# Sigmoid attention and a gated layer on one core: order of the visits, sums issued ahead, and fewer weights converted beside the attention

## The chip, the cores and the metric

The kernel runs on one core of a Trainium2 chip. A core has TensorE (PE, matmuls, and PEld for its weight loads), VectorE (DVE), ScalarE (ACT), GpSimd (POOL) and SyncE (SP), which here only issues transfers. The metric is the device time of one execution in microseconds; lower is better.

## The reference

```python
# q, k, v: (8, 12, 448, 64); w_gate, w_val: (768, 1536); w_out: (1536, 768)
scores = q @ k.T / sqrt(64) - log(448)
x = sigmoid(scores) @ v                 # per batch and head; heads joined: x is (8*448, 768)
gate = sigmoid(x @ w_gate)
y = (gate * (x @ w_val)) @ w_out        # (3584, 768)
```

The weights arrive in float64 and are converted to float32 in the kernel, from their 64-bit words.

## The kernel before, in words

**Attention.** 24 head groups `m` with 7 steps `g` each make 168 beats. In a beat TensorE makes one tile of scores (L314) and the values of an earlier one (L331); ScalarE makes the sigmoid (L317). A finished pair of heads is evicted by a ScalarE copy (L341) and a VectorE addition (L348), which frees its PSUM tile, and goes to `x_dram`.

**Conversion of weights.** `convert` is a generator of steps. A group of 12 steps (`operands`) takes four blocks of 128x384 words through integer operations on VectorE and POOL (`Words.first`, `Words.second`), forms seven operands of Strassen's product (`high`, and the four sums at L193), splits each into a high part rounded to the fp32r type (POOL, L157) and the rest as a low part (VectorE, L143), and stores it (`a_dram` for the first layer, `o_ops` for the output layer). The first layer needs 12 groups: `jp` = 0 to 5, each with `t` = 0 (gate) and 1 (value). In the attention 10 of them are done (`FIRST_JPS = 5`; 120 steps spread over 160 beats), the other two and the six groups of the output layer run beside the visits, by a table `due` that says how many steps follow each product (tick).

**Visits.** The batch of 8 is treated as 4 pairs. An "A" visit makes the first layer of a pair, a "C" visit its output layer, each by Strassen-Winograd's seven products. All visits use matmuls of 128x128 by 128x448 in fp32r, three for each product of tiles (low weight by high x, high by high, high by low).

An A visit has 12 units of 7 products, 84 products of 9 matmuls. Its operands are the seven combinations of x, as high and low parts `bh`, `bl` (`bs`). They are made by `split_x`: a cast on ScalarE (L244), a subtraction on VectorE (L217), and the sums of x on POOL (L217). `load_x` loads the next pair's x into `r` tiles beside the visit, and `split_x` for the next visit runs beside the last unit, three steps for each product. Products are added up by `plus` (L428, VectorE from PSUM, POOL from SBUF), gates are taken by ScalarE (L484), values multiplied by the gate on VectorE or POOL (L583).

A C visit has n = 0 to 6 with three products each of 18 matmuls. Its operands `hh`, `hl` are made by `Operands`: `make` runs the generator on, a cast on ScalarE (L520), a subtraction on VectorE (L217) and sums in place on POOL (L217), issued at the step before the cast of the item that needs them. `OPERANDS = 10` tiles of each kind hold them.

The hidden rows of a pair are either held in SBUF (`hold`, tiles `v`), where the C visit follows the A visit at once, or stored (`h<-g`) and read back during the C visit before (`load_hidden`, `hx<-h`, `v<-h`).

Weight operands come from memory through a ring of 8 tiles `A` (`load_operands`, L279), each loaded when the product that used its tile is done. Of the first layer's operands 15 stay resident in the `v` tiles and in `res`, loaded in the first A visit and used again in the second.

SyncE issues all transfers in program order. Every engine works through its own instructions in order; so the order in which the program emits steps is the order in each queue.

The order of visits before is the line

```python
visits = [("A", 0), ("A", 1), ("A", 2), ("C", 2), ("A", 3), ("C", 3), ("C", 1), ("C", 0)]
```

Of the kernel before, what the change touches and what calls it, by code (L numbers as in the profile page):

```python
# [9 lines left out]
F32 = mybir.dt.float32  # L10
# [8 lines left out]
P = 128  # L19
# [6 lines left out]

AHEAD, AHEAD_FF = 4, 2

FIRST_JPS = 5

LAG = 2

RING = 8
BEYOND = 3

OPERANDS = 10


@with_exitstack
def sigmoid_attention_glu_kernel(ctx: ExitStack, tc: tile.TileContext, qk, v, wg, wv, wo, out):  # L40
# [43 lines left out]
    o_ops = [dram.tile([KC, P, KH, 2, P], F32, name=f"oo{n}") for n in range(N_OPS)]  # L84
    h_dram = {}

    def chunks(jps, ks):
        res = []
        for jp in jps:
            for w in (wg, wv):  # L90
                res += [w[2 * jp + j][:, c * CW:(c + 1) * CW] for j in range(2) for c in range(2)]
        for k in ks:
            res += [wo[k + KH * half][:, c * CW:(c + 1) * CW] for c in range(2) for half in range(2)]
        return res
# [35 lines left out]
            nc.vector.scalar_tensor_tensor(out=m, in0=raw[:, :, 0], scalar=21, in1=m, op0=ALU.logical_shift_right, op1=ALU.bitwise_or)  # L130
            nc.vector.scalar_tensor_tensor(out=f, in0=m, scalar=2.0 ** -31, in1=f, op0=ALU.mult, op1=ALU.mult)  # L131

    def convert(words, jps, ks):

        pool = words.pool

        unsent, unsplit = [], []

        def split(keep):

            while len(unsplit) > keep:
                to, hl, key, sends = unsplit.pop(0)
                nc.vector.tensor_tensor(out=hl[:, 1], in0=to, in1=hl[:, 0], op=ALU.subtract)  # L143
                unsent.append((key, sends))

        def send(keep):

            while len(unsent) > keep:
                key, sends = unsent.pop(0)
                for s in sends:  # L150
                    nc.sync.dma_start(**s)
                stored.add(key)

        def high(to, where):
            key, sends = where
            hl = pool.tile([P, 2, CW], F32R, tag="whl", name="whl", bufs=words.held)
            nc.gpsimd.tensor_copy(hl[:, 0], to)  # L157
            unsplit.append((to, hl, key, sends(hl.bitcast(F32))))

        def to_a(jp, t, n):  # L160
            return ("a", jp, t, n), lambda hl: [dict(out=a_dram[jp][t][n], in_=hl)]

        def to_op(k, n):
            return ("o", k, n), lambda hl: [dict(out=o_ops[n][:, :, k, a].rearrange("o p f -> p o f"),
                                                 in_=hl[:, a].rearrange("p (o f) -> p o f", f=P)) for a in range(2)]

        def chunk(i, where, done):
            f = pool.tile([P, CW], F32, tag=f"wf{i}", name="wf", bufs=1)
            done.append(f)
            words.first(f)  # L170
            split(1)
            send(1)
            yield
            send(0)
            split(0)
            words.second()
            if where:
                high(f, where)
            yield

        def operands(to):
            fs = []
            for i, n in enumerate((0, 4, None, 6)):
                yield from chunk(i, to(n) if n is not None else None, fs)
            a11, a12, a21, a22 = fs
            split(0)

            s2 = pool.tile([P, CW], F32, tag="wf4", name="wf", bufs=1)
            for n, (x, y, z, op) in enumerate(((a22, a21, a22, ALU.add), (s2, a22, a11, ALU.subtract),
                                                (a21, a11, a21, ALU.subtract), (a12, a12, s2, ALU.subtract))):  # L190
                split(1)
                send(1)
                nc.gpsimd.tensor_tensor(out=x, in0=y, in1=z, op=op)  # L193
                high(x, to((1, 2, 3, 5)[n]))
                yield

        for jp in jps:
            for t in range(2):
                yield from operands(lambda n: to_a(jp, t, n))
        for k in ks:  # L200
            yield from operands(lambda n: to_op(k, n))
        split(0)
        send(0)
# [7 lines left out]
        return xpool.tile([P, S], F32, tag=tag, name=tag)  # L211

    pairs = list(range(B // 2))
    visits = [("A", 0), ("A", 1), ("A", 2), ("C", 2), ("A", 3), ("C", 3), ("C", 1), ("C", 0)]

    def subtract(engine, to, x, y):
        engine.tensor_tensor(out=to, in0=x, in1=y, op=ALU.subtract)  # L217
# [1 line left out]
    def load_x(pr, new):  # L219
# [4 lines left out]
            nc.sync.dma_start(out=xs[i, k], in_=x_dram[i // 2 * KC + k][:, b * S:(b + 1) * S])  # L224
            yield
        for k in range(KC):
            xs[4, k] = new()
            subtract(nc.gpsimd, xs[4, k], xs[1, k], xs[0, k])
            yield
            subtract(nc.gpsimd, xs[1, k], xs[3, k], xs[1, k])  # L230
            yield

    def split_x(cast=nc.scalar.copy):

        work = [(n, k) for n in range(N_OPS) for k in range(KC)]
        source = lambda n, k: xs[(0, 4, 4, 1, 2, 3, 4)[n], k]
        for at in range(len(work) + 2):
            if at >= 2:
                hi, lo = bs[work[at - 2]]
                subtract(nc.vector, lo, source(*work[at - 2]), hi)  # L240
            if 1 <= at <= len(work):
                n, k = work[at - 1]
                bs[n, k] = tuple(xpool.tile([P, S], F32R, tag=f"b{a}{n}{k}", name=f"b{a}") for a in "hl")
                cast(bs[n, k][0], source(n, k))  # L244
            if at < len(work):
                n, k = work[at]
                if n in (2, 6):
                    subtract(nc.gpsimd, xs[4, k], xs[3 if n == 2 else 2, k], xs[4, k])
            yield


    N_A = 2 * JPS * N_OPS
    RESIDENT = range(12, N_A, 5)
    N_HELD = 2 * KH

    def visit_operands(v_):
        kind, _ = visits[v_]
        if kind == "A":
            return [(a_dram[jp][t][n].rearrange("p a f -> p (a f)"), [("a", jp, t, n)],
                     r if r in RESIDENT and v_ < 2 else None)  # L260
                    for r, (jp, t, n) in enumerate(itertools.product(range(JPS), range(2), range(N_OPS)))]
        return [(o_ops[n][o][:, h * KC:(h + 1) * KC].rearrange("p k a f -> p (k a f)"),
                 [("o", h * KC + k, n) for k in range(KC)], None) for n in range(N_OPS) for o in range(KC) for h in range(2)]
# [26 lines left out]
    with tc.manual_schedule(), tc.tile_pool(name="att", bufs=2) as att, tc.tile_pool(name="sc", bufs=2, space=PSUM) as scp, \  # L290
# [82 lines left out]
        nc.vector.memset(zeros, 0.0)  # L373
        load_first()
        warm_up(2)
        words = Words(att, chunks(range(FIRST_JPS), ()), AHEAD, 4)
        weights, n_weights, done = convert(words, range(FIRST_JPS), ()), 24 * FIRST_JPS, 0

        first_x = 2 * NQ + 1
        tags = iter(SUMS)  # L380
        x_loads = load_x(0, lambda: sb(next(tags)) if len(xs) < len(SUMS) else att.tile([P, S], F32, tag=f"xt{len(xs)}", name="xt", bufs=1))
        splits = split_x(nc.gpsimd.tensor_copy)
        beat = 0
        for m in range(B * NQ):
# [29 lines left out]


    hid = ctx.enter_context(tc.tile_pool(name="hid", bufs=1, reuse_waits="tile"))
    rawx = ctx.enter_context(tc.tile_pool(name="rawx", bufs=1, reuse_waits="tile"))
    un = ctx.enter_context(tc.tile_pool(name="un", bufs=8, space=PSUM, reuse_waits="tile"))

    later = []  # L420
# [79 lines left out]
    class Operands:  # L500
# [6 lines left out]
        def steps(self):  # L507
# [4 lines left out]
            for at in range(len(self.items) + 2):  # L512
                if at >= 2:
                    item = self.items[at - 2]
                    subtract(nc.vector, hb[item][1], source(*item), hb[item][0])
                if 1 <= at <= len(self.items):
                    assert at - 1 < self.used + OPERANDS
                    item = self.items[at - 1]
                    hb[item] = tuple(oper[0].tile([P, S], F32R, tag=f"h{a}", name=f"h{a}", bufs=OPERANDS) for a in "hl")
                    nc.scalar.copy(hb[item][0], source(*item))  # L520
                if at < len(self.items):
                    pr, n, k = self.items[at]
                    b = [hs.get((pr, i, k)) for i in range(4)]
                    sums = {1: (b[0], b[1], b[0]), 2: (b[0], b[3], b[0]), 3: (b[1], b[3], b[1]), 6: (b[0], b[2], b[0])}
                    if n in sums:
                        subtract(nc.gpsimd, *sums[n])
                yield

        def make(self, to):
# [7 lines left out]

    def new_raw():
        raw_names[0] += 1
        return rawx.tile([P, S], F32, tag=f"r{raw_names[0] % (5 * KC)}", name="r")  # L540

    def a_visit(v_):

# [10 lines left out]
        def tick():  # L554
# [7 lines left out]
            if p >= N_A - 6:  # L562
                for _ in range(3):
                    next(splits, None)
                if keep:
                    chain[0].make(min(2 * (p - (N_A - 7)), OPERANDS + 1))
            beside(v_, p)

        for jp in range(JPS):
# [27 lines left out]
    def load_hidden(pr):  # L597

        def new(at):
            if visits[-1][1] == pr:  # L600
                return held(at).bitcast(F32)
            return [xpool.tile([P, S], F32, tag=f"b{a}{at // KC}{at % KC}", name="hx") for a in "hl"]

# [8 lines left out]
    def c_visit(v_):  # L612
# [14 lines left out]
        for n in range(N_OPS):  # L627
            ops.make(ops.used + KH + 2)
            for o in range(KC):
# [13 lines left out]
                    nc.scalar.copy(p5, acc)  # L643
                elif n == 2:
                    plus(u2, acc, p1)
                    plus(u4, u2, p5, nc.gpsimd)
                elif n == 3:
                    plus(u2, acc, u2)
                    plus(p5, u2, p5, nc.gpsimd)
                    send(1, 1, p5)  # L650
                elif n:
                    to, m, t = {4: (p1, 0, 0), 5: (u4, 0, 1), 6: (u2, 1, 0)}[n]
                    plus(to, acc, to)
                    send(m, t, to)
                if o < KC - 1:
                    ops.make(ops.used + OPERANDS + o)
                next(splits, None)
                if steps % 6 == 0:
                    next(splits, None)
# [8 lines left out]
    stage = ExitStack()  # L668
    stage.enter_context(tc.manual_schedule())
    conv = stage.enter_context(tc.tile_pool(name="conv", bufs=1, reuse_waits="tile"))  # L670
    res = stage.enter_context(tc.tile_pool(name="res", bufs=1, reuse_waits="tile"))

    def make_resident():
# [4 lines left out]

    new_resident[0] = make_resident

    words = Words(conv, chunks(range(FIRST_JPS, JPS), range(KH)), AHEAD_FF, 3)
    weights = convert(words, range(FIRST_JPS, JPS), range(KH))
    n_first, n_second = 24 * (JPS - FIRST_JPS), 12 * KH
    last_conv = 2
    quiet = [t for v_ in range(last_conv) for t in range(N_A * (v_ + 1) - 7, N_A * (v_ + 1) + 8)]
    firsts = range(5, 49)
    seconds = [t for t in range(49, N_A * (last_conv + 1) - 16) if t not in quiet]
    due = {}
    for ticks, n in ((firsts, n_first), (seconds, n_second)):
        for i, t in enumerate(ticks):  # L690
# [54 lines left out]
```

## Time and profile before

| | |
|---|---|
| median of 3 runs | 1235.29 us (1234.97 to 1235.72) |
| the profiled execution | 1232.44 us, its span 1230.7 us |
| mean granted TensorE clock | 0.992 |
| busy, share of the span | PE 97%, weight loads 80%, DVE 65%, ACT 34%, POOL 49% |
| matmuls | 2688 records in the attention, 4536 in the visits, 16 to warm up |
| transfers | 359.60 MB, mean 292 GB/s |

Places in the span (us): attention to 270; A0 270 to 427; A1 427 to 587; A2 587 to 746; C2 746 to 833; A3 to 991; C3 to 1071; C1 to 1151; C0 to the end. Tables by stretch give, for each window, its length, then each engine's busy time with the number of its records in brackets, the granted clock, the share of the transfer engines and their rate. In rows of groups the numbers behind the bar are busy time, the mean of one in ns, and the idle time of the engine before them with what ended it.

### The profile page before, as it was taken

How to read it: one execution, taken by the hardware profiler on the slowest of the kernel's cores; microseconds unless marked ns; L12 is line 12 of the kernel's file. 1: busy time of each engine (PE TensorE's matmuls, PEld its weight loads, DVE VectorE, ACT ScalarE, POOL GpSimd, SP SyncE). 2: the span in 40 equal slices, each digit the busy share in tenths (PEclk: the TensorE clock that was granted, in tenths of full speed). 3: DMA queues.
4: the chain of work that ended last, by engine and by line, in shares of the span. 5: the costliest groups of instructions: out<-in, count | busy, mean ns of one | idle time of the engine just before them, and what ended most of it. 6: DMA issues, size and time to landing. Idle time of an engine off the chain costs nothing. (4 is left out here: it accounts for less than half of the span.)

```text
span 1230.7 us, 20521 instructions
## 1 busy us (share of the span) xinstructions
PE 1199.8 (97%) x7240; PEld 983.8 (80%) x7240; DVE 805.7 (65%) x1208; ACT 423.7 (34%) x664; POOL 608.8 (49%) x607
## 2 busy tenths in 40 slices
PE   9999999999999989999999999899999999999998
PEld 4444464459999979999899998789999998988988
DVE  6887789956688586877776756763232466556563
ACT  6777676561111321122311224421112233233231
POOL 3334556544564644654648438632222277353651
PEclk9999999999999999999999999889999999999999
DMA  9999999989999769999699997578777788989876
GB/s 324 359 367 410 328 330 312 332 283 353 398 353 370 238 246 367 296 319 300 231 377 312 302 280 209 161 222 255 217 214 217 216 267 283 355 279 321 290 201 195
DMA packets 168343, 359.60 MB, mean 292 GB/s; under 512 B 16305, under 2 KB 79409, under 8 KB 168241
## 3 DMA queue, kind: packets, MB, share of 16 engines
q1 hardware_dynamic: 168240, 358.28, 87.4%
q8 instruction: 58, 0.95, 0.3%
q14 instruction: 45, 0.36, 0.1%
HBM read 275.64 MB, written 82.58 MB: 291 GB/s over the span
## 5 line engine op out<-in xcount | busy, mean ns | idle before, releaser
L443 PE MATMUL un<-bh,A 128*128 128x448 f32 x1836 | 523.9, 367 | 0.0
L443 PEld LDWEIGHTS un<-bh,A 128*128 128x128 f32 x1836 | 345.6, 188 | 29.8 <-issue 0.7
L443 PE MATMUL un<-bl,A 128*128 128x448 f32 x918 | 337.3, 367 | 5.8 <-DVE bl L217 5.8
L443 PE MATMUL un<-hh,A 128*128 128x448 f32 x1008 | 290.6, 370 | 4.9 <-ACT hh L520 4.9
L331 PE MATMUL av<-a,v 64*64 64x448 f32 x1344 | 208.3, 540 | 7.1 <-DVE x L348 7.0
L443 PEld LDWEIGHTS un<-hh,A 128*128 128x128 f32 x1008 | 192.0, 191 | 21.1 <-ACT hh L520 6.1
L314 PE MATMUL sc<-qk 64*64 64x448 f32 x1344 | 207.0, 541 | 0.4 <-ACT a L317 0.4
L317 ACT ACTIVATE a<-sc,bias 128x896 f32<-128x896 f32 x168 | 169.3, 1009 | 78.3 <-PE sc L314 67.9
L443 PE MATMUL un<-hl,A 128*128 128x448 f32 x504 | 188.7, 374 | 7.6 <-DVE hl L217 7.5
L443 PEld LDWEIGHTS un<-bl,A 128*128 128x128 f32 x918 | 172.8, 188 | 22.9 <-DVE bl L217 8.5
L157 POOL CAST whl<-wf 128x384 fp32r<-128x384 f32 x126 | 71.7, 569 | 176.4 <-DVE wf L131 119.7
L428 POOL TENSOR_TENSOR u<-u,p 128x448 f32<-128x448 f32 x48 | 57.2, 1192 | 197.0 <-DVE u L428 196.7
L217 DVE TENSOR_TENSOR hl<-v,hh 128x448 fp32r<-128x448 f32 x126 | 120.4, 989 | 32.3 <-ACT hh L520 27.3
L331 PEld LDWEIGHTS av<-a,v 64*64 64x64 f32 x1344 | 76.9, 134 | 69.4 <-issue 49.7
L314 PEld LDWEIGHTS sc<-qk 64*64 64x64 f32 x1344 | 75.9, 134 | 69.3 <-issue 55.4
L143 DVE TENSOR_TENSOR whl<-wf,whl 128x384 fp32r<-128x384 f32 x126 | 111.8, 891 | 25.5 <-POOL whl L157 25.3
L484 ACT ACTIVATE g<-c 128x448 f32<-128x448 f32 x96 | 52.6, 575 | 201.3 <-DVE c L428 169.2
L443 PEld LDWEIGHTS un<-hl,A 128*128 128x128 f32 x504 | 95.9, 190 | 23.4 <-DVE hl L217 16.0
L217 POOL TENSOR_TENSOR v<-v 128x448 f32<-128x448 f32 x72 | 99.8, 1413 | 22.1 <-DVE hl L217 21.1
L520 ACT CAST hh<-v 128x448 fp32r<-128x448 f32 x126 | 67.8, 567 | 113.0 <-PE un L443 66.8
L456 ACT COPY p<-un 128x448 f32<-128x448 f32 x48 | 25.4, 529 | 224.2 <-PE un L443 203.0
L428 DVE TENSOR_TENSOR u<-un,p 128x448 f32<-128x448 f32 x48 | 29.8, 622 | 98.2 <-PE un L443 97.4
(70 smaller groups left out, 1239.0 us busy)
## 6 DMA issues: line engine op xcount, KB each, us to landing
A<-ad SPq DMA_DIRECT2D x306, 384.0 KB, 4.8
A<-oo SPq DMA_DIRECT2D x168, 384.0 KB, 4.1
ad<-whl SPq DMA_DIRECT2D x84, 384.0 KB, 6.4
qk<-qk SPq DMA_DIRECT2D x23, 896.0 KB, 7.4
oo<-whl SPq DMA_DIRECT2D x84, 192.0 KB, 5.6
v<-vv SPq DMA_DIRECT2D x24, 448.0 KB, 6.8
xd<-x SPq DMA_DIRECT2D x48, 224.0 KB, 6.9
h<-g SPq DMA_DIRECT2D x48, 224.0 KB, 4.8
```

The costliest lines, as they stand in the source:

```text
L143: nc.vector.tensor_tensor(out=hl[:, 1], in0=to, in1=hl[:, 0], op=ALU.subtract)
L157: nc.gpsimd.tensor_copy(hl[:, 0], to)
L217: engine.tensor_tensor(out=to, in0=x, in1=y, op=ALU.subtract)
L314: nc.tensor.matmul(sc[halves[u], h, :S], lhsT=qkt[halves[h], p, k0:k0 + HP], rhs=qkt[halves[h], p, :S], start=True, stop=True)
L317: nc.scalar.activation(a, sc[:, :, :S], AF.Sigmoid, bias=bias, scale=scale)
L331: nc.tensor.matmul(avs[key][halves[h], :S], lhsT=vt[halves[u], g, h], rhs=a[halves[u], h], start=start, stop=g == last)
L428: engine.tensor_tensor(out=to, in0=x, in1=y, op=ALU.add)
L443: nc.tensor.matmul(acc, lhsT=w, rhs=m, start=i == 0, stop=i == len(terms) - 1)
L456: nc.scalar.copy(p1, next_product(0))
L484: nc.scalar.activation(gates[i], acc, AF.Sigmoid)
L520: nc.scalar.copy(hb[item][0], source(*item))
```

## The change

The visits are now A0, A1, A2, A3, C3, C2, C1, C0. Only pair 3 is held; pairs 0 to 2 are stored and read back. The resident operands are 13 and are used in three visits. In the attention nine groups of weights are converted (`FIRST = 9`, counted by `jp` and `t`), three are left for the first visit (36 steps over ticks 5 to 61); the steps of the output layer are spread to the end of A3. The sums of x get a tile more for each `k` (`xs[5]`), made in `load_x`, and the sum for n = 6 is emitted right after the low part of n = 2. In `Operands` the sums are emitted right after the low part that read the tile last, six or twelve items ahead; 16 tiles of each kind let `make` run further, two items for each product. The POOL additions for the output are emitted one product later (`later`).

```diff
-FIRST_JPS = 5
+FIRST = 9
...
-OPERANDS = 10
+OPERANDS = 16
...
-    visits = [("A", 0), ("A", 1), ("A", 2), ("C", 2), ("A", 3), ("C", 3), ("C", 1), ("C", 0)]
+    visits = [("A", pr) for pr in pairs] + [("C", pr) for pr in reversed(pairs)]
...
         for k in range(KC):
-            xs[4, k] = new()
+            xs[4, k], xs[5, k] = new(), new()
             subtract(nc.gpsimd, xs[4, k], xs[1, k], xs[0, k])
+            yield
+            subtract(nc.gpsimd, xs[5, k], xs[3, k], xs[4, k])
             yield
...
-        source = lambda n, k: xs[(0, 4, 4, 1, 2, 3, 4)[n], k]
+        source = lambda n, k: xs[(0, 4, 5, 1, 2, 3, 5)[n], k]
...
-                subtract(nc.vector, lo, source(*work[at - 2]), hi)
+                n, k = work[at - 2]
+                subtract(nc.vector, lo, source(n, k), hi)
+                if n == 2:
+                    subtract(nc.gpsimd, xs[5, k], xs[2, k], xs[5, k])
...
-            if at < len(work):
-                n, k = work[at]
-                if n in (2, 6):
-                    subtract(nc.gpsimd, xs[4, k], xs[3 if n == 2 else 2, k], xs[4, k])
...
-    RESIDENT = range(12, N_A, 5)
+    RESIDENT = range(12, 77, 5)
...
-                     r if r in RESIDENT and v_ < 2 else None)
+                     r if r in RESIDENT and v_ < len(pairs) - 1 else None)
...
                     subtract(nc.vector, hb[item][1], source(*item), hb[item][0])
+                    pr, n, k = item
+                    b = [hs.get((pr, i, k)) for i in range(4)]
+                    for to, x, y in {0: ((0, 1, 0),), 1: ((0, 3, 0), (1, 3, 1)), 2: ((0, 2, 0),)}.get(n, ()):
+                        subtract(nc.gpsimd, b[to], b[x], b[y])
...
-                if at < len(self.items):
-                    pr, n, k = self.items[at]
-                    b = [hs.get((pr, i, k)) for i in range(4)]
-                    sums = {1: (b[0], b[1], b[0]), 2: (b[0], b[3], b[0]), 3: (b[1], b[3], b[1]), 6: (b[0], b[2], b[0])}
-                    if n in sums:
-                        subtract(nc.gpsimd, *sums[n])
...
-                    chain[0].make(min(2 * (p - (N_A - 7)), OPERANDS + 1))
+                    chain[0].make(min(2 * (p - (N_A - 7)), 12))
...
-                    plus(u4, u2, p5, nc.gpsimd)
+                    later.append(lambda u4=u4, u2=u2, p5=p5: plus(u4, u2, p5, nc.gpsimd))
...
-                    plus(p5, u2, p5, nc.gpsimd)
-                    send(1, 1, p5)
+                    later.append(lambda u2=u2, p5=p5: plus(p5, u2, p5, nc.gpsimd))
+                    unsent.append((steps + 3, out[o + KC, :, (2 * pr + 1) * S:(2 * pr + 2) * S], p5))
...
-                if o < KC - 1:
-                    ops.make(ops.used + OPERANDS + o)
+                ops.make(min(ops.made + 2, ops.used + OPERANDS + 1))
...
-    n_first, n_second = 24 * (JPS - FIRST_JPS), 12 * KH
-    last_conv = 2
+    n_first, n_second = 12 * (2 * JPS - FIRST), 12 * KH
+    last_conv = len(pairs) - 1
...
-    firsts = range(5, 49)
-    seconds = [t for t in range(49, N_A * (last_conv + 1) - 16) if t not in quiet]
+    firsts = range(5, 62)
+    seconds = [t for t in range(62, N_A * (last_conv + 1) - 16) if t not in quiet]
```

More of the change, by code (lines that the diff above doesn't have):

```diff
@@ L85, in sigmoid_attention_glu_kernel, with chunks @@
     h_dram = {}
-    def chunks(jps, ks):
+    halves_of_jps = list(itertools.product(range(JPS), range(2)))
+    def chunks(parts, ks):
         res = []
-        for jp in jps:
-            for w in (wg, wv):
-                res += [w[2 * jp + j][:, c * CW:(c + 1) * CW] for j in range(2) for c in range(2)]
+        for jp, t in parts:
+            res += [(wg, wv)[t][2 * jp + j][:, c * CW:(c + 1) * CW] for j in range(2) for c in range(2)]
         for k in ks:
@@ L131, in second, with convert @@
             nc.vector.scalar_tensor_tensor(out=f, in0=m, scalar=2.0 ** -31, in1=f, op0=ALU.mult, op1=ALU.mult)
-    def convert(words, jps, ks):
+    def convert(words, parts, ks):
         pool = words.pool
@@ L195, in operands @@
                 yield
-        for jp in jps:
-            for t in range(2):
-                yield from operands(lambda n: to_a(jp, t, n))
+        for jp, t in parts:
+            yield from operands(lambda n: to_a(jp, t, n))
         for k in ks:
@@ L375, in sigmoid_attention_glu_kernel, with new_x @@
         warm_up(2)
-        words = Words(att, chunks(range(FIRST_JPS), ()), AHEAD, 4)
-        weights, n_weights, done = convert(words, range(FIRST_JPS), ()), 24 * FIRST_JPS, 0
+        words = Words(att, chunks(halves_of_jps[:FIRST], ()), AHEAD, 4)
+        weights, n_weights, done = convert(words, halves_of_jps[:FIRST], ()), 12 * FIRST, 0
         first_x = 2 * NQ + 1
-        tags = iter(SUMS)
-        x_loads = load_x(0, lambda: sb(next(tags)) if len(xs) < len(SUMS) else att.tile([P, S], F32, tag=f"xt{len(xs)}", name="xt", bufs=1))
+        tags = itertools.chain(SUMS, (f"xt{i}" for i in range(2 * KC)))
+        def new_x():
+            tag = next(tags)
+            return sb(tag) if tag in SUMS else att.tile([P, S], F32, tag=tag, name="xt", bufs=1)
+        x_loads = load_x(0, new_x)
         splits = split_x(nc.gpsimd.tensor_copy)
@@ L416, in sigmoid_attention_glu_kernel @@
     hid = ctx.enter_context(tc.tile_pool(name="hid", bufs=1, reuse_waits="tile"))
-    rawx = ctx.enter_context(tc.tile_pool(name="rawx", bufs=1, reuse_waits="tile"))
+    raw_pool = [None]
     un = ctx.enter_context(tc.tile_pool(name="un", bufs=8, space=PSUM, reuse_waits="tile"))
@@ L539, in new_raw @@
         raw_names[0] += 1
-        return rawx.tile([P, S], F32, tag=f"r{raw_names[0] % (5 * KC)}", name="r")
+        return raw_pool[0].tile([P, S], F32, tag=f"r{raw_names[0] % (6 * KC)}", name="r")
     def a_visit(v_):
@@ L599, in new @@
         def new(at):
-            if visits[-1][1] == pr:
+            if pr % 2:
                 return held(at).bitcast(F32)
@@ L670, in sigmoid_attention_glu_kernel @@
     conv = stage.enter_context(tc.tile_pool(name="conv", bufs=1, reuse_waits="tile"))
+    raw_pool[0] = stage.enter_context(tc.tile_pool(name="rawx", bufs=1, reuse_waits="tile"))
     res = stage.enter_context(tc.tile_pool(name="res", bufs=1, reuse_waits="tile"))
@@ L679, in sigmoid_attention_glu_kernel @@
     new_resident[0] = make_resident
-    words = Words(conv, chunks(range(FIRST_JPS, JPS), range(KH)), AHEAD_FF, 3)
-    weights = convert(words, range(FIRST_JPS, JPS), range(KH))
-    n_first, n_second = 24 * (JPS - FIRST_JPS), 12 * KH
-    last_conv = 2
+    words = Words(conv, chunks(halves_of_jps[FIRST:], range(KH)), AHEAD_FF, 3)
+    weights = convert(words, halves_of_jps[FIRST:], range(KH))
+    n_first, n_second = 12 * (2 * JPS - FIRST), 12 * KH
+    last_conv = len(pairs) - 1
     quiet = [t for v_ in range(last_conv) for t in range(N_A * (v_ + 1) - 7, N_A * (v_ + 1) + 8)]
-    firsts = range(5, 49)
-    seconds = [t for t in range(49, N_A * (last_conv + 1) - 16) if t not in quiet]
+    firsts = range(5, 62)
+    seconds = [t for t in range(62, N_A * (last_conv + 1) - 16) if t not in quiet]
     due = {}
```

## The prediction

> **What bounds the kernel now.** I read the waits of TensorE first, then busy time by stretch, then the timeline around each stretch that loses time. TensorE waits for no transfer; it waits for VectorE and ScalarE, a few microseconds at a time.
>
> ```profile
> engine line waited for: us in total, times, longest us
> PE un L443 <- DVE hl L217: 7.5, 9, 2.0
> PE av L331 <- DVE x L348: 7.0, 7, 2.9
> PE un L443 <- DVE bl L217: 5.8, 6, 2.1
> PE un L443 <- ACT hh L520: 4.9, 4, 1.6
> ```
>
> Busy time hides more: a record lasts 367 ns although matmuls start about 203 ns apart, so a late start still counts as busy. In the stretches below (length; then busy time and, in brackets, records) I count records instead.
>
> ```profile
> core 0: us, PE busy (x) PEld busy (x) DVE busy (x) ACT busy (x) POOL busy (x), PEclk, DMA share, GB/s
> 30.00:125.00 95.00, 95.00 (x1017) 46.00 (x1013) 75.50 (x143) 71.20 (x82) 41.22 (x60) 1.00 1.01 379
> 125.00:230.00 105.00, 97.92 (x993) 51.21 (x989) 90.21 (x152) 69.13 (x79) 59.76 (x79) 0.98 0.95 321
> ...
> 270.70:427.00 156.30, 156.30 (x758) 142.00 (x757) 107.37 (x168) 29.15 (x56) 80.48 (x86) 1.00 0.95 344
> 427.00:446.00 19.00, 15.48 (x63) 12.46 (x63) 18.60 (x25) 7.95 (x17) 11.72 (x10) 0.91 0.39 132
> ...
> 590.00:601.00 11.00, 8.70 (x42) 7.42 (x41) 10.93 (x15) 3.60 (x8) 5.92 (x4) 1.00 0.34 116
> 601.00:745.00 144.00, 144.00 (x713) 133.43 (x712) 95.03 (x146) 28.42 (x55) 80.24 (x82) 1.00 0.96 316
> 745.00:836.00 91.00, 83.68 (x375) 73.72 (x374) 61.37 (x74) 30.76 (x61) 47.97 (x35) 0.92 0.71 202
> ...
> 991.00:1071.00 80.00, 78.21 (x381) 70.72 (x379) 46.15 (x59) 24.48 (x46) 44.88 (x34) 1.00 0.92 302
> 1071.00:1151.00 80.00, 78.27 (x381) 70.87 (x380) 46.82 (x59) 25.31 (x48) 42.11 (x31) 1.00 0.93 312
> 1151.00:1227.00 76.00, 74.26 (x361) 67.13 (x360) 41.31 (x50) 21.35 (x41) 35.70 (x26) 1.00 0.72 218
> ```
>
> About two records of a window hang over its edges. So 601:745 is the undisturbed pace: 144/711 = 0.2025 us per matmul. In 30:125 the attention makes 1017/95 = 10.7 records per us. Lost against these paces: attention 125:230, 105 - 993/10.7 = 12.2; visit A0 (270.7:427), 156.3 - 756 x 0.2025 = 3.2, which is not a wait but a slower pace of 0.2067; boundary A0 to A1 (427:446), 19 - 61 x 0.2025 = 6.6; A1 to A2, 11 - 40 x 0.2025 = 2.9; the output visit C2 with both its edges (745:836), 91 - 373 x 0.2025 = 15.5; C3, C1 and C0, 80 - 379 x 0.2025 = 3.3, again 3.3, and 76 - 359 x 0.2025 = 3.3. Together 50.3 of the span of 1230.7; the matmuls themselves are not touched by the change.
>
> **The change part by part.**
>
> *Nine half-blocks converted in the attention instead of ten.* The waits there are for L348, an addition that frees a PSUM tile and stands in VectorE's queue behind conversion work:
>
> ```profile
> 219.26 0.85 DVE L143 TENSOR_TENSOR whl<-wf,whl 128x384 fp32r<-128x384 f32 x1
> 220.03 0.71 DVE L128 TENSOR_SCALAR wf<-wf 128x384 uint32<-128x384 uint32 x1
> ...
> 222.31 0.62 DVE L348 TENSOR_TENSOR x<-av,x 128x448 f32<-128x448 f32 x1
> ```
>
> ```profile
> 222.99 0.60 PE L331 MATMUL av<-a,v 64*64 64x448 f32 x2 [2.91 <-DVE x L348]
> ```
>
> Cost of one conversion step: in 30:125 VectorE is busy 75.5, of which L348 is
>
> ```profile
> L348 DVE TENSOR_TENSOR x<-av,x 128x448 f32<-128x448 f32 x18 | 11.2, 620 | 9.7 <-ACT x L341 9.7
> ```
>
> so 64.3 us for 95/1.503 = 63.2 beats x 120/160 steps = 47.4 steps, 1.36 us each (a beat is 16 records, 16/10.7 = 1.5 us). With 108 steps the 70 beats of 125:230 carry 70 x 12/160 = 5.2 steps fewer: 7.1 us off VectorE, which is 86% busy there. If each microsecond came back to TensorE the gain would be 7.1; the burst of ordered work keeps part. Three more sums of x (xs[5]) are made in the loading phase, three fewer in the splitting phase: no net work. I take -5.5, ends 0 and -10.
>
> *The twelve steps go to visit A0.* First conversions now run 36 steps in 57 products instead of 24 in 44, the rest thinner (72 in 213 ticks instead of 72 in 157). Up to 386 us that is 36 steps where about 30 stood: 6 x 1.36 = 8.2 us more of VectorE, and 6 x 11/12 x 0.393 MB = 2.2 MB more.
>
> ```profile
> 275.00:386.00 111.00, 111.00 (x539) 100.83 (x538) 82.45 (x128) 17.79 (x34) 62.17 (x67) 1.00 1.00 371
> 92.00:123.00 31.00, 31.00 (x336) 15.02 (x332) 23.46 (x42) 23.16 (x27) 14.99 (x21) 1.00 1.03 410
> ```
>
> VectorE goes from 74% to (82.45 + 8.2)/111 = 82%. That is near the 86% at which the attention loses time, but here eight PSUM tiles of one product (1.86 us) each lie between TensorE and a late VectorE. The transfers go from 371 to (41.2 + 2.2)/111 = 391 GB/s; the attention's row shows 410 moved without a wait. I take 0, with a far end of +12 below. The Trainium skill, "DMA: Bandwidth & Descriptors", section Where 436 GB/s comes from, says that about 358 GB/s of HBM per core binds; the two rows, 371 and 410, disagree. By that page the stretch would need 43.4 MB/358 = 121 us, 10 to 12 us late.
>
> *Sums of x ahead (split_x).* At an A-to-A boundary the split for the next visit runs beside the last unit. Its sums for n=6 are issued in place, on POOL, behind a product by the gate that itself waited 3.9 us for VectorE:
>
> ```profile
> 593.12 1.47 POOL L583 TENSOR_TENSOR g<-c,g 128x448 f32<-128x448 f32 x1 [3.90 <-DVE c L428]
> 594.55 4.49 POOL L217 TENSOR_TENSOR r<-r 128x448 f32<-128x448 f32 x3
> ```
>
> ```profile
> 596.11 0.57 ACT L244 CAST bh<-r 128x448 fp32r<-128x448 f32 x1 [5.08 <-POOL r L217]
> ```
>
> ScalarE waits 5.1 us for them, VectorE's bl follows, TensorE stands. After the change n=2's sums are done long before (they are xs[5]), n=6's are queued four products earlier: six POOL sums in that window become three. The three that vanish also free VectorE, because bl beside a POOL operation takes up to 1589 ns where the median is 620:
>
> ```profile
> L217 DVE TENSOR_TENSOR bl<-r,bh x63: 610/620/1589, 420.0 to 831.8; 128x448 fp32r<-128x448 f32 x63
> ```
>
> 3 x 0.95 = 2.9 us, and the waits of ScalarE before it (5.1, and a like one for n=2) go. What is late next: bl of n=5 at A2, needed about 596.6; replaying the queue with 0.54 us for a free bl and 1.5 for a crossed one gives about 597.0. So some tenths stay: 1.5 us at A0 to A1, where conversions leave ScalarE behind, 1.0 at A1 to A2. Of 9.5, 7.0 goes; ends -3 and -9.5. The Trainium skill, "SBUF — State Buffer", section Who interferes with whom, calls the port between these engines an exclusive lock: whichever comes second blocks entirely. By that each vanished sum frees its whole 1.14 us, 3.4 instead of 2.9; the row agrees in kind.
>
> *All A visits, then all C.* C2 in the middle had to split x for A3 and prepare its own operands at once, through the same three engines:
>
> ```profile
> ACT hh L520 <- POOL v L217: 9.4, 6, 5.4
> ...
> PE un L443 <- DVE hl L217: 5.6, 6, 2.0
> ```
>
> That visit kind is gone; A2 to A3 becomes a boundary of the kind just costed (1.0). Its 15.5 becomes 1.0: -14.5, ends -12 and -15.5. Price: A2 is no longer held, so 24 more rows stored and 24 more read (48 x 0.229 = 11 MB) and 13 instead of 15 resident tiles, now for three visits. The reads fall in one more output visit of the kind of 991:1071 and 1071:1151, which carry them at 302 and 312 GB/s with no wait of TensorE for a transfer; the stores fall in A2, whose conversion thins. 0.
>
> *Sums of operand tiles ahead (Operands, 16 tiles, `later`).* In an output visit the sums for n=3 are issued one step before their cast and stand behind the additions for the output:
>
> ```profile
> 1098.26 1.53 POOL L428 TENSOR_TENSOR c<-g,p 128x448 f32<-128x448 f32 x1
> 1099.76 1.15 POOL L217 TENSOR_TENSOR hx<-hx 128x448 f32<-128x448 f32 x1
> 1101.58 1.41 POOL L428 TENSOR_TENSOR g<-g,u 128x448 f32<-128x448 f32 x1 [0.68 <-ACT hh L520]
> 1102.95 1.52 POOL L217 TENSOR_TENSOR hx<-hx 128x448 f32<-128x448 f32 x1
> ```
>
> ```profile
> 1104.50 1.97 ACT L520 CAST hh<-hx 128x448 fp32r<-128x448 f32 x4 [3.00 <-POOL hx L217]
> ```
>
> Now a sum goes out with the previous low part, six or twelve items before its use, the output additions go one product later, and operands may run 15 items (2.5 n) ahead instead of 11. Twelve sums of 1.5 us fall in one n of 11 us (54 matmuls), so POOL lags by 7 us and recovers in the next n; the cast that needs the first is 9 us away. 9.9 us lost in three visits becomes 0.3 in each of four: -8.7, ends -5 and -9.9. Behind the waiting cast on ScalarE stand only copies of sums with eight PSUM tiles of slack.
>
> *A3 to C3.* In the last six products of A3 twelve steps instead of eleven issue 14 sums instead of 5, all before the first C product. 9 x 0.95 = 8.6 us more of VectorE in the 23 us from the first of these sums to the last operand that n=1 needs (five A products of 1.86 and some 67 C matmuls); the low parts of n=1 come out just in time. +1.5, ends 0 and +4. Behind these sums on POOL queues the product by the gate for the last hidden rows, used 11 us later.
>
> Sum: -5.5 + 0 - 7.0 - 14.5 + 0 - 8.7 + 1.5 = -34.2. The profiled execution took 1232.44, the median of the runs is 1235.29, 2.85 above; on the median 1201.
>
> **The rivals.** *Pace.* A0 starts matmuls 0.2067 apart; behind the waits of 427:446 the pace is 0.2025 (601:745) and stays so. If the boundaries lose their waits altogether the slow pace may last through A1 to A3: 3 x 756 x 0.0042 = 9.5, less the 3.5 of waits that I had left: 1207; to the very end 16 - 4.7, 1212. For: no wait interrupts A0. Against: the replay leaves small waits, and a wait was followed by the fast pace. *Attention unmoved:* the order of VectorE's queue, not its load, decides: 1206.5. For: 14% of VectorE is idle there. *Crossing instead of waiting:* sums behind each low part run beside the next one at 1.5 us, so boundaries keep half (4.7 instead of 2.5, 3 instead of 1) and output visits 5 instead of 1.2: 1209. *Better:* near the floor of 50 us, 1190. *Slower than before:* A0's first 59 products become bound by transfers. It must lose over 34.2, that is move 43.4 MB below 43.4/(111 + 34.2) = 299 GB/s. Against it stands the landing time of A tiles from 275 to 433 us:
>
> ```profile
> DMA to landing us min/median/max: 3.1/5.8/8.5
> ```
>
> Operand loads of A0 land in 8.5 us at most, and are issued seven products (13 us) ahead. Short of that, 1212.
>
> **How the numbers follow.** Forecast 0.50, pace 0.15, crossing 0.14, attention unmoved 0.11, transfers in A0 0.06 (half of it slower than before), better 0.04. 0.2% is 2.5 us, what a measurement tells here. Faster 0.95, same 0.02, slower 0.03. The range 1190 to 1216 takes in pace, crossing and attention, and two of their prices together.
>
> **What would show it.** ScalarE's wait for POOL's r and v or hx (L217) nearly gone; no TensorE wait for hh; windows of about 77 us per output visit; a clean A2 to A3; L348's waits in the attention about halved; transfers of A0's first 110 us near 390 GB/s. The prediction is wrong if A0 shows waits for A tiles, if matmuls start 0.2067 apart beyond A0, if bl and hl stay at 1.5 us around the boundaries, or if C3 starts with a wait of over 4 us.

## The result and the profile after

The changed kernel took 1197.64 us in the median of four runs (1188.78, 1191.71, 1203.58, 1203.89); the kernel before 1235.13. The ratio is 0.9698, 95% interval 0.9617 to 0.9779. Six more runs of the same kernel later gave 1188.12, 1188.60, 1188.99, 1190.88, 1190.94 and 1203.32 (ratio 0.9656, 0.9616 to 0.9696). So the times lie in two groups, 1188 to 1192 and 1203 to 1204, and the median of the four falls between them. The profiled execution (1188.78, span 1186.9) is of the lower group.

Its waits of TensorE, whole:

```profile
engine line waited for: us in total, times, longest us
PE sc L370 <- DVE zeros L374: 1.4, 1, 1.4
PE av L332 <- DVE x L349: 1.0, 1, 1.0
PE un L449 <- DVE c L434: 0.6, 1, 0.6
PE sc L315 <- ACT a L318: 0.4, 1, 0.4
PE un L449 <- DVE bl L217: 0.3, 1, 0.3
```

Of the 25 us in the rows shown of before 1.9 is left (without `zeros` and `sc`, waits of the first 7 us), and none is for `hh` or `hl`. By stretch, at the same places of the program as before (attention, A0 to A3, C3, C2, C1):

```profile
core 0: us, PE busy (x) PEld busy (x) DVE busy (x) ACT busy (x) POOL busy (x), PEclk, DMA share, GB/s
125.00:220.00 95.00, 94.02 (x1000) 38.73 (x994) 82.12 (x132) 69.63 (x80) 60.71 (x76) 1.00 0.95 333
...
260.00:361.00 101.00, 100.88 (x490) 91.14 (x486) 74.57 (x111) 14.60 (x27) 56.24 (x59) 1.00 0.96 355
361.00:426.00 65.00, 64.47 (x318) 59.76 (x319) 60.26 (x90) 22.01 (x45) 37.77 (x39) 1.00 0.90 330
426.00:580.00 154.00, 153.66 (x759) 142.09 (x758) 105.30 (x155) 35.16 (x69) 79.84 (x77) 1.00 0.89 290
580.00:733.00 153.00, 153.00 (x757) 141.65 (x756) 101.16 (x151) 34.97 (x69) 79.10 (x77) 1.00 0.89 291
733.00:886.00 153.00, 153.00 (x756) 141.63 (x755) 93.37 (x142) 32.24 (x62) 74.04 (x72) 1.00 0.89 279
886.00:963.00 77.00, 77.00 (x382) 71.35 (x381) 51.07 (x61) 25.45 (x49) 48.97 (x36) 1.00 0.94 323
963.00:1040.00 77.00, 77.00 (x382) 71.35 (x381) 47.75 (x59) 25.23 (x48) 41.88 (x31) 1.00 0.95 325
1040.00:1117.00 77.00, 77.00 (x382) 71.35 (x381) 47.69 (x58) 25.22 (x48) 41.85 (x31) 1.00 0.95 321
```

Counted as in the prediction, an output visit holds 380 matmuls in 77 us, 0.2026 each: nothing is lost. The boundaries of the A visits lose 0.7 at 426 us and 0.1 behind it. The attention loses 95 - 1000/10.7 = 1.5 instead of 12.2. What is left stands in A0: 488 matmuls in the 101 us up to 361 us, 0.207 each, and one wait at the end of that row. The span fell by 43.8: 10.5 up to the start of A0 (270.7 to 260.2), 33.3 behind it.

### The profile page after: what moved, and what is told of

Its sections match the earlier page's. It is cut to its first block, busy times and chain, and to the rows that moved or that the text cites. A ratio compares the mean times of both kernels' runs of the same rounds, so it can differ in the third digit from the quotient of the medians.

```text
span 1186.9 us, 20654 instructions
## 1 busy us (share of the span) xinstructions
PE 1179.6 (99%) x7240; PEld 959.2 (81%) x7240; DVE 808.4 (68%) x1208; ACT 421.7 (36%) x664; POOL 607.2 (51%) x607
## 4 chain that ended last, share of the span: by engine, by line
PE 90%; DVE 3%; POOL 3%; DMA 2%; issue 1%; ACT 0%; SPq 0%; POOLq 0%; DVEq 0%
PE un L449 70%; PE av L332 10%; PE sc L315 10%; DVE bl L217 1%; DMA r<-xd 1%; DMA ad<-whl 1%; POOL r L217 1%; DMA h<-g 1%; POOL wf L194 0%; DVE wf L129 0%; DMA qk<-qk 0%; DVE wf L130 0%; POOL whl L158 0%; POOL g L587 0%; DVE wm L131 0%
## 5 line engine op out<-in xcount | busy, mean ns | idle before, releaser
L449 PE MATMUL un<-bh,A 128*128 128x448 f32 x1782 | 507.1, 366 | 0.6 <-DVE c L434 0.6
L449 PE MATMUL un<-bl,A 128*128 128x448 f32 x891 | 325.9, 366 | 0.3 <-DVE bl L217 0.3
L332 PE MATMUL av<-a,v 64*64 64x448 f32 x1344 | 175.4, 536 | 1.0 <-DVE x L349 1.0
L315 PE MATMUL sc<-qk 64*64 64x448 f32 x1344 | 175.4, 538 | 0.4 <-ACT a L318 0.4
L315 PEld LDWEIGHTS sc<-qk 64*64 64x64 f32 x1344 | 59.5, 133 | 78.4 <-issue 65.8
L332 PEld LDWEIGHTS av<-a,v 64*64 64x64 f32 x1344 | 59.8, 133 | 70.9 <-issue 66.7
L217 DVE TENSOR_TENSOR hl<-v,hh 128x448 fp32r<-128x448 f32 x84 | 85.2, 1052 | 14.3 <-ACT hh L530 14.1
L217 POOL TENSOR_TENSOR hx<-hx 128x448 f32<-128x448 f32 x48 | 65.6, 1397 | 45.0 <-DVE hl L217 45.0
L217 DVE TENSOR_TENSOR hl<-hx,hh 128x448 fp32r<-128x448 f32 x84 | 78.5, 972 | 11.7 <-ACT hh L530 11.7
L194 POOL TENSOR_TENSOR wf<-wf 128x384 f32<-128x384 f32 x72 | 77.9, 1082 | 12.8 <-DVE whl L144 6.8
```

Of the source, the lines that this page charges most:

```text
L315: nc.tensor.matmul(sc[halves[u], h, :S], lhsT=qkt[halves[h], p, k0:k0 + HP], rhs=qkt[halves[h], p, :S], start=True, stop=True)
L332: nc.tensor.matmul(avs[key][halves[h], :S], lhsT=vt[halves[u], g, h], rhs=a[halves[u], h], start=start, stop=g == last)
L449: nc.tensor.matmul(acc, lhsT=w, rhs=m, start=i == 0, stop=i == len(terms) - 1)
```

## Experiments

Each kernel is the changed one with the edit shown, if nothing else is said.

**The changed kernel again, and one wait added.**

> The changed kernel once more. Its four runs were 1188.8, 1191.7, 1203.6 and 1203.9 us; the profiled one (1188.8) started A0 at 206.7 ns per matmul, met its first wait at 360 us and ran at 202.7 ns from there. Theory P (pace): the spread is that pace. A run in which no wait breaks the slow pace costs up to 3780 x 4.0 ns = 15 us more. Expected: times in two groups, 1188 to 1192 and 1203 to 1204; if the profiled run is of the upper group its windows show 242 matmul records per 50 us to the end instead of 248. Rival R (transfers or something else from outside): the spread stays but a slow run shows single waits, or is slow in some stretches only, and records per 50 us stay at 248 elsewhere.

```diff
+    pause = [lambda: subtract(nc.vector, bs[4, 0][1], xs[2, 0], bs[4, 0][0])]
...
         plus(u3, next_product(3), u2)
+        if pause:
+            pause.pop()()
```

> The changed kernel with one more VectorE subtraction in A0, which writes the low part of one x operand (n=4, k=0) a second time behind the addition of product 3, so that the fifth product of A0 has to wait once, about 1 us. Theory P: this wait breaks the slow pace 7 us into A0 in every run: all runs 1186 to 1190 us, no upper group, 0.99 of the changed kernel's mean; the profile shows 248 records per 50 us from 270 us on. Rival R: the time is 1 us longer than the changed kernel's and has the same two groups.

`one_wait` took 1188.83, 1190.05, 1199.01, 1201.54, 1206.54 and 1206.55. Its profiled execution is one of the slowest. Three windows of TensorE, first of it, then of the changed kernel's first profile (length, busy time, records):

```profile
280.00:330.00 50.00, 50.00 (x249) 1.00 0.99 376
450.00:500.00 50.00, 50.00 (x243) 1.00 0.94 308
1100.00:1150.00 50.00, 50.00 (x244) 1.00 0.91 299
```

```profile
280.00:330.00 50.00, 50.00 (x244) 1.00 1.00 372
450.00:500.00 50.00, 50.00 (x248) 1.00 0.93 308
1100.00:1150.00 50.00, 50.00 (x249) 1.00 0.85 256
```

The granted clock is full in all six, and there are two paces, 242 and 247 matmuls in 50 us (two records hang over the edges). The changed kernel went from the slow to the fast one at its wait at 361 us. `one_wait` was fast from A0's start, before and behind the wait I gave it (268 us), and turned slow at a wait at 360 us, until its end 840 us later. So the second half of theory P fell: a wait doesn't give the fast pace; behind it the pace can be either of the two. That the pace makes the two groups fits: from the boundary A0 to A1 on 3780 matmuls at 4.0 ns more are 15.1 us, and the groups lie 15 apart. But both profiles of the changed kernel are of the lower group; a slow pace up to the end was seen in the profiles of its variants `one_wait` (1206.55) and `sums_in_place` (1204.64).

**The kernel before with the same wait.**

> The kernel before with the same added subtraction in A0. Theory P: A0 runs at 202.7 instead of 206.7 ns, 3.0 us less, the wait costs 1 us: about 1233.3 us against 1235.3. Rival R: 1236.3 us.

1235.70 us in the median (12 runs, 1230.86 to 1239.85; ratio 1.0009, 0.9988 to 1.003): no gain. In its profile A0 has the slow pace behind the added wait too, and leaves it at A1; the other eleven executions were not profiled:

```profile
300.00:350.00 50.00, 50.00 (x243) 1.00 1.00 376
450.00:500.00 50.00, 50.00 (x248) 1.00 1.02 353
```

Over the 14 profiles I counted every stretch of 14 or more matmuls of the visits between two waits: the first stretch, at the start of A0, was slow in 10 of 14; a stretch behind a wait in 13 of 100. Each stretch kept one pace, 202.7 or 206.7 ns. The kernel before has some 17 stretches in an execution, the changed one five, the last of which is half of the visits' matmuls.

**The order of visits alone.**

> The changed kernel's order of visits (with its three stored pairs, 13 resident tiles and conversions up to A3) with the rest undone: ten half-blocks in the attention, x sums in place, ten operand tiles, operand sums in place, additions at once; and the added subtraction of the run one_wait. By the sum in the prediction the order is worth 14.5 - 1.5 = 13 us: against the kernel before with the wait (1233.3) about 1221 us, with 3 us lost at each boundary between A visits and 3 us in each of the four output visits. Rival (the order alone only moves the loss: each C visit and the third A boundary lose as much as C2 did): 1230 us or more.

```diff
 # the changed kernel with these back as before, and the wait of one_wait added:
+FIRST = 10; firsts = range(5, 49); OPERANDS = 10
+source = lambda n, k: xs[(0, 4, 4, 1, 2, 3, 4)[n], k]      # x sums in place
+subtract(nc.gpsimd, *sums[n])                              # operand sums in place
+plus(u4, u2, p5, nc.gpsimd)                                # at once
```

1225.79 us in the median (11 runs; ratio 0.9945, 0.9922 to 0.9968), 9.9 below `before_wait` and 7.8 below the kernel before in the same rounds (1233.58), where the sum said 12 to 13. The places where it loses are those expected:

```profile
425.00:444.00 19.00, 16.70 (x74) 0.91 0.58 184
590.00:604.00 14.00, 11.92 (x51) 0.88 0.55 185
750.00:761.00 11.00, 8.71 (x35) 0.84 0.52 176
...
979.00:1059.00 80.00, 78.26 (x382) 1.00 0.93 314
```

4.4, 4.1 and 4.3 us at the three A boundaries (19 - 72 x 0.2025 and so on), 3 in an output visit. The 15.5 of the old C2 became one such boundary and one such visit, 7.4, so by these windows the order alone gains 8.1.

**Ten half-blocks in the attention.**

> The changed kernel with ten half-blocks of weights converted in the attention again, two beside A0 (24 steps in 44 ticks). By the prediction's first term the attention's end moves from 259.7 us to later by 5.5 us; as measured from kernel to kernel it moved by 10.5 us (270.2 to 259.7), so if the number of steps alone made that, A0 starts at 270 us; if half of it came from the x sums' other order, at 264 to 266. The wait in A0 near 360 us goes if the dense conversion caused it.

```diff
-FIRST = 9
+FIRST = 10
...
-    firsts = range(5, 62)
-    seconds = [t for t in range(62, ...
+    firsts = range(5, 49)
+    seconds = [t for t in range(49, ...
```

```profile
PE av L332 <- DVE x L349: 10.3, 6, 2.9
PE sc L370 <- DVE zeros L374: 1.4, 1, 1.4
PE sc L315 <- ACT a L318: 0.4, 1, 0.4
```

It took 1198.85, 1201.12, 1212.24 and 1219.37 us; the profile is of the longest. A0 starts at 275.9 us there, later than either value expected, 15.7 later than with nine and 5.2 later than in the kernel before; `order_alone`, which has ten and the old x sums, starts it at 271.0. `x_sums_in_place`, below, has nine and the old x sums and starts it at 259.2. So twelve steps are worth 11.8 us with the old order of the x sums and 15.7 with the new one, which itself costs 4.9 us of attention beside ten half-blocks and 1.0 beside nine (259.2 to 260.2). The 15.7 and the 4.9 stand on this one profile. The three rows are all its waits: A0 waits no more, so the wait needs the dense conversion; and with no wait behind A0's slow start this execution ran its 4536 matmuls at 206.7 ns. At 4.0 ns more for each that is 18.1 us, which is about what parts it from the two shortest runs.

**x loaded later, and later with the added wait; x loaded earlier.**

> The changed kernel with the next pair's x loaded and summed from product 34 of a visit instead of product 8, so that POOL's nine sums of x in A0 fall behind the 36 dense conversion steps. The changed kernel waits once in A0, 1.0 to 2.8 us at 359 to 361 us, for an addition of VectorE that is eight products late. Theory V (VectorE and POOL are overfull in ticks 5 to 61 of A0): the wait goes, 1 to 2.5 us less. Theory D (each wait draws the pace anew, 202.7 or 206.7 ns, mostly the first; the start of A0 drew 206.7 in 4 of 6 profiles): with the wait at 360 gone A0 keeps the pace of its start to 426 us, and where no wait follows to the end: more runs near 1203 us than of the changed kernel, the others at 1186 to 1189. Rival: the wait comes from the number of conversions, wherever the x sums are; it stays and the times are those of the changed kernel.

> The run x_late with the added VectorE subtraction that makes the fifth product of A0 wait about 1 us. Theory D: the draw behind that wait is mostly the fast pace, as it was in 70 of 78 stretches between waits: median 1186 to 1188 us with one run in eight or so at 1202 to 1204; without the wait (x_late) the upper group is larger. Rival (the pace is not drawn at waits but set by the execution as a whole): the same share of slow runs with and without the added wait.

> The changed kernel with the next pair's x loaded and summed in every product from the eighth on instead of every second: POOL's nine sums of x end at product 28 of A0 (about 312 us) instead of product 48 (349 us). Theory V: the wait of A0 near 360 us is VectorE's queue meeting these sums and the dense conversion; with the sums early it goes, and the boundary A0 to A1 stays as in the changed kernel (0.5 us): the fast runs at 1186 to 1188 us, 1 to 3 us below those of the changed kernel. Rival: the wait moves to near 312 us or to the boundary, as it moved to 419 to 429 us when the sums were made later; no gain. For both, runs that keep or draw the slow pace lie 9 to 18 us higher.

```diff
-            if p >= 8 and p % 2 == 0:
+            if p >= 34 and p % 2 == 0:      # x_late, x_late_wait
+            if p >= 8:                      # x_early
                 next(x_loads, None)
```

`x_late` took 1197.38 us in the median (1191.09 to 1201.50), `x_late_wait` 1193.65 (1192.86 to 1208.28), `x_early` 1192.82 (1189.33 to 1203.68). The waits of the visits in `x_late`, then the longest in `x_early`:

```profile
PE un L449 <- DVE bl L217: 4.0, 4, 2.1
```

```profile
PE un L449 <- DVE u L434: 1.8, 1, 1.8
```

In `x_late` the wait of A0 is gone and 4.0 us stand at the boundary (419 to 429 us) instead; in `x_early` it moved to 330 to 338 us, 1.8 and 0.3. For `x_late` neither theory V nor its rival holds, since the wait neither went nor stayed but moved; for `x_early` the rival was right. In an A0 that carries 36 dense steps a wait stands wherever POOL's sums were put here. On theory D they tell little: the profiled `x_late` was fast from A0's start and turned slow at 735 us; with the added wait 2 of 6 runs lay high, without it 3 of 6. That is too few to tell the two apart.

**x sums in place.**

> The changed kernel with the sums of x for n=2 and n=6 issued in place at the boundary between A visits, as before. Theory X (the early sums removed the waits of these boundaries): A0 to A1, A1 to A2 and A2 to A3 wait 2.5 to 6 us each again, TensorE for bl, 9 to 14 us together. Rival (fewer conversions at the end of a visit did it): the boundaries stay under 1 us each.

Windows over its three A boundaries (the same places lose at most 0.7 us each in the changed kernel):

```profile
420.00:433.00 13.00, 10.91 (x46) 0.87 0.56 184
578.00:591.00 13.00, 10.71 (x46) 0.87 0.56 188
736.00:746.00 10.00, 7.69 (x37) 1.00 0.47 154
```

13 - 44 x 0.2025 = 4.1, again 4.1, and 10 - 35 x 0.2025 = 2.9: 11.1 us, with conversions as thin as in the changed kernel (its times: 1194.66, 1198.37, 1198.38 and 1206.42). Theory X holds. Behind the longest wait of each of the first two, 2.2 us, matmuls start about 373 ns apart for some 3 us (granted clock 0.57 in 428:432), which is about 1.5 us of the 4.1; behind the third, of the same length, the clock stays full.

**The three edits of the output visits, apart.**

> The changed kernel with the operand sums of the output visits issued one step before the cast that needs them, as before; 16 operand tiles and the later additions stay. Theory S (the early place of the sums removes the waits of the output visits): each output visit loses 2 to 3 us again, TensorE waiting for hh and hl at n=3, visits of 79 to 80 us instead of 76.6. Rival (the run-ahead of 15 items or the later additions suffice): visits stay at 76.6 to 77 us.

> The changed kernel with operand sums in place and the additions of the output at once; of the third part only the 16 operand tiles and the longer run-ahead stay. Theory L (the run-ahead alone hides POOL's order): output visits without waits of TensorE, 76.6 us each at the fast pace or 78.1 at the slow. Rival (the additions one product later matter): waits for hh at n=3 of 1 to 3 us in each output visit.

> The changed kernel with ten operand tiles and the run-ahead of before; the operand sums stay early and the additions late. Theory L: the shorter run-ahead lets waits of 1 to 3 us come back in each output visit. Rival (the early place of the sums suffices): visits without waits.

```diff
 # sums_in_place: the sums one step before the cast, 16 tiles and later additions kept
 # only_16: also the additions at once
 # ten_operands: OPERANDS = 10 and the old make(...), early sums and later additions kept
```

`only_16` took 1189.34 us in the median (1188.68 to 1203.63); its output visits C3 and C2, then two of `ten_operands`:

```profile
887.00:964.00 77.00, 77.00 (x382) 71.35 (x381) 52.82 (x61) 26.80 (x52) 51.35 (x37) 1.00 0.96 324
964.00:1041.00 77.00, 77.00 (x382) 71.35 (x381) 45.88 (x58) 24.39 (x48) 41.47 (x32) 1.00 0.94 325
```

```profile
969.00:1047.00 78.00, 78.00 (x380) 70.88 (x380) 46.47 (x58) 25.58 (x48) 41.97 (x31) 1.00 0.95 319
1047.00:1124.00 77.00, 77.00 (x377) 70.16 (x377) 45.47 (x57) 25.58 (x48) 40.96 (x31) 1.00 0.94 319
```

With 16 tiles alone nothing is lost, at the fast pace. ScalarE waits longer there for POOL's sums than in the kernel before, 54.1 us for `v` and 43.7 for `hx`, and TensorE still has no wait for `hh` or `hl`. With ten tiles, the early sums and the later additions a visit loses 78 - 378 x 0.2025 = 1.5 or 77 - 375 x 0.2025 = 1.1, against 3.3 with none of the three; `ten_operands` took 1194.61, 1195.59, 1197.00 and 1204.07 us, its three shortest 6 to 9 us above the shortest of the changed kernel. `sums_in_place` (1190.66, 1204.04, 1204.64, 1207.96) lost nothing either, but its profile ran at the slow pace, which leaves 1.5 us of slack in a visit. So the longer run-ahead is sufficient for the output visits; the early sums and the later additions together take away over half of the loss where it is missing, and add nothing on top of it that these runs show. No run has the early sums without the later additions.

None of these versions beats the changed kernel by more than the two paces scatter it: 1189.3 for `only_16`, 1197.6 and 1189.9 for the changed kernel.

## Why the prediction was right, and where it was not

1201 was forecast, 1190 to 1216 for the range; 1197.64 lies within, and the direction was right. But the sum was for one profiled execution, and there 43.8 us went instead of 34.2. That the median of the four came near 1201 was luck: two of them lay in the upper group, 15 us above the others, for which the sum has no term and only the rival *pace* has one. In the six later runs one lay there, and their median, 1189.93, is just below the range.

- *Attention*, -5.5 with ends 0 and -10: measured -10.5, outside its own ends. The mis-sized step is the bound of "7.1 if each microsecond came back to TensorE": 5.2 steps fewer freed more than their own time. VectorE's share does not decide it: it is 86% in both rows (90.21/105 and 82.12/95), with 12.2 us lost in one and 1.5 in the other. That VectorE's queue falls behind in bursts is my reading, which no run isolates here. The lower clock behind the longest wait (0.98 in the old row, 1.00 in the new) went with the waits. That the x sums cost no net work was wrong by 1 us: 259.2 in `x_sums_in_place`, 260.0 to 261.1 in the nine profiles with nine half-blocks and the new sums.
- *Twelve steps into A0*, 0: a new wait at 360 us, 0.8 us beyond the pace in the first profile, 2.6 in the second and 2.3 in that of `one_wait`, for an addition that empties a PSUM tile eight products old. Here is VectorE just before it, then the same three lines a few microseconds later: 0.35 and 0.56 us become 1.3 to 1.5 beside POOL. Its rows stand last, three beside the long operations and one with POOL's idle time (2.40 us) during the short ones:

```profile
356.19 1.29 DVE L129 TENSOR_SCALAR wf<-wf 128x384 uint32<-128x384 uint32 x1 [0.40 <-POOL wf L119]
357.52 1.40 DVE L130 SCALAR_TENSOR_TENSOR wf<-wraw,wf 128x384 uint32<-128x384 uint32 x1
358.84 1.50 DVE L131 SCALAR_TENSOR_TENSOR wm<-wraw,wm 128x384 uint32<-128x384 uint32 x1
360.38 0.56 DVE L132 SCALAR_TENSOR_TENSOR wf<-wm,wf 128x384 f32<-128x384 uint32 x1
360.85 0.62 DVE L434 TENSOR_TENSOR c<-un,p 128x448 f32<-128x448 f32 x1
```

```profile
363.84 0.35 DVE L129 TENSOR_SCALAR wf<-wf 128x384 uint32<-128x384 uint32 x1
364.22 0.56 DVE L130 SCALAR_TENSOR_TENSOR wf<-wraw,wf 128x384 uint32<-128x384 uint32 x1
364.70 0.55 DVE L131 SCALAR_TENSOR_TENSOR wm<-wraw,wm 128x384 uint32<-128x384 uint32 x1
```

```profile
356.12 1.15 POOL L434 TENSOR_TENSOR u<-u,p 128x448 f32<-128x448 f32 x1
357.22 1.28 POOL L434 TENSOR_TENSOR c<-u,p 128x448 f32<-128x448 f32 x1
358.46 1.47 POOL L217 TENSOR_TENSOR r<-r 128x448 f32<-128x448 f32 x1
365.90 0.57 POOL L158 CAST whl<-wf 128x384 fp32r<-128x384 f32 x1 [2.40 <-DVE wf L132]
```

Here is the stretch for which 82% and 391 GB/s were forecast, taken from the same point of A0:

```profile
264.50:375.50 111.00, 110.35 (x536) 100.15 (x535) 86.77 (x132) 17.36 (x33) 64.28 (x69) 1.00 0.97 355
```

VectorE was busy 86.77/111 = 78% of it, 74% up to 361 us (74.57/101) and 93% from there to 426 us (60.26/65); the average says nothing of the burst. The transfers were not it: no wait of TensorE is for one, and 355 GB/s moved instead of 391. So this row does not test the limit of about 358 of "DMA: Bandwidth & Descriptors", section Where 436 GB/s comes from, in the Trainium skill; the window 280:330 does, with 372 GB/s and no wait of TensorE.
- *A boundaries*, 7.0 of 9.5, with 3.5 left at three: 0.7 to 0.8 left. The mechanism is shown by `x_sums_in_place`; ScalarE's wait for POOL's sums of x (`bh` for `r`) is 28.4 us in the kernel before, 6.1 in the changed one and 34.4 there. My replay kept too much of the crossing with POOL.
- *Order*, -14.5: the visit of 15.5 is gone. `order_alone` shows that by itself the order leaves 7.4 in its place; the rest came with the other edits.
- *Output visits*, -8.7: -9.9. The size was nearly right, the cause was not: I gave most of it to the early sums, and the longer run-ahead does it alone. ScalarE still waits for POOL's sums of operand tiles, 22.0 and 13.6 us where I had expected it nearly gone, and the 16 tiles absorb it. First the kernel before, then the changed one:

```profile
ACT hh L520 <- POOL v L217: 44.5, 20, 5.4
ACT hh L520 <- POOL hx L217: 10.5, 4, 4.9
```

```profile
ACT hh L530 <- POOL v L217: 22.0, 11, 4.0
ACT hh L530 <- POOL hx L217: 13.6, 8, 2.9
```

- *A3 to C3*, +1.5: 0, at the low end: no two matmuls start over 0.21 us apart from 734 us to the last one.
- *Pace* had a chance of 0.15 as a whole-kernel outcome. Three of the ten runs of this kernel lay in the upper group, which the sign "matmuls 0.2067 apart beyond A0" had named. The mechanism, fewer waits and so a pace that lasts, is seen in `one_wait`, `sums_in_place` and `ten_halves`; my reading that a wait gives the fast pace is refuted.

## What to carry to other kernels

Where engines in order feed TensorE, a few more tiles of run-ahead can do what a careful order of the queue does, and can be tried first. Judge a tuned kernel's waits by records in a window, not by busy time or averages: an engine busy 78% of a stretch still stalled TensorE in a burst. When the last waits are gone, look at the spread of the runs before the median: they may form two groups, and a median between them belongs to neither.

## What the runs showed of the hardware that was not expected

Matmuls of 128x128 by 128x448 in fp32r, each with its own weight load of 188 ns, start either 202.7 or 206.7 ns apart at the same full granted clock. The pace holds unchanged between two waits (4535 matmuls in `ten_halves`) and can change at a wait: slow in 13 of 100 stretches behind one, in 10 of 14 at the first one after the attention. The slow pace seems to last also because it is slow: at 206.7 the small waits at the A boundaries, where it could change, did not occur in `one_wait`, `sums_in_place` and `ten_halves`. What sets it is open; no run here changed the start of a stretch in a controlled way. The page "TensorE: Matmul & The Clock Gate" of the Trainium skill, section Wait — 56ns, not 53.3ns?, gives N/2.4 + 2.5 ns for warm matmuls, 189 ns here; neither pace is that.
